# Recurrent attention and a channel-mixing layer in one kernel: decay scans in four parts, early bf16 fillers, late guards and a rewritten order

## The chip, the cores and the metric

One core of one Trainium2 chip. The metric is device microseconds (us) of one execution of the whole program. TensorE (PE) multiplies matrices into PSUM; VectorE (DVE), ScalarE (ACT) and GpSimd (POOL) do the elementwise work; the queue of SyncE (SP) issues all DMA transfers.

## The reference

Four batches, 8 heads, 768 time steps, head dimension 48. A linear recurrence with a decay gives `x`; a low-rank mix over time is added; two dense layers with a ReLU follow. All of it is float32.

```python
for t in range(S):                                   # S = 768
    cur = einsum('bhd,bhe->bhde', u[None] * kt, vt)
    y[:, :, t] = einsum('bhd,bhde->bhe', rt, state + cur)
    state = wt[..., None] * state + einsum('bhd,bhe->bhde', kt, vt)
x = y.transpose(0, 2, 1, 3).reshape(B, S, H * D)     # (4, 768, 384)
h = x.transpose(0, 2, 1) @ U @ V                     # U (768, 32), V (32, 768)
u = x + h.transpose(0, 2, 1)
out = u + maximum(u @ w_ch1, 0.0) @ w_ch2            # 384 -> 1536 -> 384
```

## The kernel before, in words

**Chunks.** Time is cut into 24 chunks of 128 steps (6 of each batch, `g` is 0 to 23). On the chip the recurrence of a chunk becomes matmuls. `chunk(g)` lays out the steps of one chunk. The decays `w` come as a 128 x 517 tile: four groups (head pairs) of 128 columns, each with a separator column in front. One scan over the whole tile (step `F`, `scan_f`, L380) multiplies the decays from the back; a second tile, `resets`, is 1 at the separators and 0 elsewhere and starts each group anew. Step `R` writes reciprocals of the four totals into the separator columns of `qd`, and a second scan over 516 columns (step `Q`, `scan_q`, L393) multiplies from the front. Step `T` keeps the totals, `RP` multiplies r by Q, `KS` multiplies k by F. `AM` (scores), `CP` (a predicated copy that merges the scores below a diagonal made by `SEL` and `SEL2`), `YA` and `YZ` (outputs from the chunk and from the state) follow. The state: `KT` and `KN` turn k, `DS` multiplies it with v into the PSUM tile `dS`, `ZA` adds the old state, `ZM` decays it. `XE` and `XN` take PSUM results to SBUF around the transposes `XT`. In batch 0 `PR`, `MD`, `DV` make the diagonal, in the others `RK`, `RU`, `RED`. `GUARD` (`check_w`, L409) reads the decays once more and counts those out of range; a branch at the end of the program reads the counts.

**Weights.** float64 weights come as raw tiles (`LRAW`) and are rebuilt as two tiles that the fast matmul format holds, a high and a low part: `AB`, `E`, `SG` (ACT, some on DVE), `C1`, `C2`, `ADD` (DVE, some on POOL), `HI` (ACT), `SUB` (POOL or DVE). There are 12 pieces of `w1`, 12 of `w2`, and one each of U and V.

**Dense layers.** Per batch and half of the time steps: 12 up projections (`UP`, 9 matmuls of 128x384 each, L782) and 12 parts of the down projection (`DN`, 9 matmuls each, L817); 96 of each in all, so 192 steps that are called dense steps below. `HH` and `HL` take the high and low part of the ReLU out of PSUM. The first of them needs all of batch 0's recurrence and its time mix: `GW` (6 parts) into `gb`, then `GS`, `GSL`, `IX`, `HP`, `UHP`, `ULP`, `XU`.

**Order.** Nothing is left to a scheduler. `ORDER` is a string with three characters for each step: two digits of base 64 are the step's number, the third says which of two engines takes it (odd: the step's `alt`) and, halved, how many units of filler matmuls go ahead of it (`warm`, L176: two units are one 128x512 matmul on a tile `busy`, an odd one is a 128x256 matmul; results are thrown away). `plan` (L122) reads it. Each engine runs its steps in that order, and a step waits until its inputs are there and its buffer is free.

Read out, the string has the first `UP` at place 373 of 1433. Ahead of it stand, by engine:

| engine | steps ahead of the first UP, before |
|---|---|
| DVE | F 9, Q 8, R 8, CP 8, PR 6, KS 5, RP 8, C1 16, C2 16, HI 1, ADD 10, SUB 6, SUBV 2, ZM 5, ZA 4, RK 2, RU 1, RED 2, GSL 1, ULP 3, UADD 1, DV 1 |
| ACT | GUARD 8, AB 16, E 16, SG 14, HI 11, SEL 5, SEL2 5, KN 7, XE 7, XN 6, T 8, DV 5, ZM 1, HIV 2, GS 1, UHP 3, XU 3 |
| POOL | KS 3, SEL 3, SEL2 3, ADD 4, SUB 6, RK 1, RU 1 |
| PE | MD 6, KT 7, AM 8, DS 7, YA 7, YZ 5, XT 6, GW 6, VM 2, IX 3, HP 4, and 95 filler units |

`busy` is the last part of the tile for the low half of `w2`, filled from `resets` by a conversion (L172); fillers can be placed until the step `GW 0.5`.

Of the kernel before, what the change touches and what calls it, by code (L numbers as in the profile page):

```python
# [39 lines left out]
def channel_order():  # L40
# [18 lines left out]
    "5y05405+06945s05E05A01D00Q05B14w01E05x10R00S05-04s02R01S08O05u05114t05F01F11k05v00m00o06A04-01G15C05D06015d6"
    "5e05J65w00p08R01z06115Z01H01I10q15G20r11+08T01-08Y05a18o05H02A06228X05b15c02006305K08y05Q05L04x04y02C05t18U0"  # L60
    "8Z00s00t02S05fC2B01U05h05I06B02D05M22T05g05N02E15i01T08P08z15r08a15j08p08b05k05l09h05m01V08W18V08Q06C02I09O0"
    "8r02a08c11W02U08t05n05o06408d16506602F02V08g08u01X18q06701Y06802W16D08v06E06F06G08+02K06H09g00I08e08f08x06I0"
    "6M01Z08S16J08-06N00J02X16R06S08w09208h09309008i02Y19409j08s18j06O06P06K06L06V02Z06T06U08k06Q09609P11a09F07M0"
# [979 lines left out]
```

## Time and profile before

| what | us |
|---|---|
| three runs: median (lowest, highest) | 459.84 (459.72, 462.23) |
| the profiled execution: span from the first to the last instruction | 458.4 |
| its own time beside the runs | the span is 1.4 below the median of the runs |
| busy: PE, DVE, ACT, POOL | 442.2, 296.7, 175.1, 104.5 |

Busy time is the time in which an engine had at least one instruction under way. Matmuls overlap, so a row's duration is longer than its share of the stream: 9 matmuls of 128x384 last 0.34 us each and follow each other in 1.59 us. On the other engines too the next instruction starts a little before the one in front has ended; the time from one start to the next is what an instruction takes of its engine.

### The profile page before, as it was taken

Reading aid. Unit: us, or ns where it says so; the run is one execution under the profiler, and the core shown is the slowest. Engines: PE = TensorE matmul, PEld = TensorE weight load, DVE = VectorE, ACT = ScalarE, POOL = GpSimd, SP = SyncE. Lnnn points to the kernel's source line nnn. Section 1 sums busy time; section 2 is a strip of 40 time slices with the busy share of each in tenths; the row PEclk is TensorE's granted clock in tenths of the full one; section 3 lists DMA queues with packets and bytes.
Section 4 is the critical chain, followed back from the end, with each engine's and each line's share of the span. In section 5 each row is a group of like instructions: output and inputs, shape, how many; then the busy total and the mean of one; then the engine's idle time right before and its main releaser. Section 6 shows DMA issues by size and latency. Waiting matters only on the chain.

```text
span 458.4 us, 9721 instructions
## 1 busy us (share of the span) xinstructions
PE 442.2 (96%) x4066; PEld 409.9 (89%) x4066; DVE 296.7 (65%) x529; ACT 175.1 (38%) x434; POOL 104.5 (23%) x99
## 2 busy tenths in 40 slices
PE   4998899999999999999999999999999999999996
PEld 3675668999999899899999799999998899999995
DVE  7998998999989584865865675672445235402511
ACT  5998997888545221333017100141122100101100
POOL 0222645343461160113522303222000010000000
PEclk9999999999999999999999999999999999999999
DMA  8946771584424524232414212041000000010001
GB/s 271 378 133 216 281 238 61 177 288 160 147 76 127 180 62 115 67 90 82 147 42 167 59 61 64 20 123 54 23 18 1 1 17 19 2 39 31 0 3 54
DMA packets 20497, 46.95 MB, mean 102 GB/s; under 512 B 2400, under 2 KB 8928, under 8 KB 20448
## 3 DMA queue, kind: packets, MB, share of 16 engines
q1 hardware_dynamic: 20448, 46.28, 30.4%
q8 instruction: 33, 0.54, 0.5%
q14 instruction: 16, 0.13, 0.1%
HBM read 41.55 MB, written 4.72 MB: 101 GB/s over the span
## 4 chain that ended last, share of the span: by engine, by line
PE 85%; DVE 7%; ACT 3%; DMA 2%; issue 1%; SPq 1%; DVEq 0%; ACTq 0%
PE f L782 33%; PE f L817 33%; PE aps L507 4%; PE y L566 2%; PE trk L495 2%; PE y L576 2%; PE trx L626 2%; PE y L589 1%; PE dS L517 1%; DMA rk<-in_rkT 1%; DVE A L510 1%; PE hp L723 1%; PE ga L649 1%; DVE Q L395 1%; PE idle L178 1%
## 5 line engine op out<-in xcount | busy, mean ns | idle before, releaser
L782 PE MATMUL f<-u,w1h 128*128 128x384 f32 x576 | 150.1, 341 | 0.7 <-ACT xT L745 0.7
L782 PEld LDWEIGHTS f<-u,w1h 128*128 128x128 f32 x576 | 103.7, 188 | 1.3 <-ACT xT L745 1.0
L817 PE MATMUL f<-hh,w2h 128*128 128x384 f32 x288 | 99.1, 344 | 0.0
L782 PE MATMUL f<-u,w1l 128*128 128x384 f32 x288 | 97.5, 339 | 0.0
L817 PE MATMUL f<-hh,w2l 128*128 128x384 f32 x288 | 97.4, 338 | 0.0
L817 PE MATMUL f<-hl,w2h 128*128 128x384 f32 x288 | 97.0, 337 | 0.0
L795 DVE SCALAR_TENSOR_TENSOR hl<-f,hh 128x384 fp32r<-128x384 f32 x96 | 52.4, 553 | 41.0 <-ACT hh L789 39.8
L789 ACT ACTIVATE hh<-f 128x384 fp32r<-128x384 f32 x47 | 23.1, 494 | 142.7 <-PE f L782 142.6
L817 PEld LDWEIGHTS f<-hh,w2h 128*128 128x128 f32 x288 | 54.1, 188 | 1.2 <-DVE hl L795 0.6
L817 PEld LDWEIGHTS f<-hl,w2h 128*128 128x128 f32 x288 | 54.5, 189 | 0.4
L782 PEld LDWEIGHTS f<-u,w1l 128*128 128x128 f32 x288 | 54.0, 188 | 0.0
L817 PEld LDWEIGHTS f<-hh,w2l 128*128 128x128 f32 x288 | 54.0, 187 | 0.0
L791 DVE TENSOR_SCALAR hh<-f 128x384 fp32r<-128x384 f32 x49 | 27.1, 554 | 33.4 <-PE f L782 33.4
L832 DVE TENSOR_TENSOR xT<-f,xT 128x384 f32<-128x384 f32 x24 | 13.0, 550 | 36.9 <-PE f L817 36.9
L510 DVE COPY_PREDICATED A<-maskf,aps 128x1024 f32<-128x1024 uint32 x24 | 32.7, 1361 | 2.8 <-PE aps L507 2.4
L445 ACT ACTIVATE A<-ident,dv 128x128 f32<-128x128 f32 x108 | 34.0, 394 | 1.2 <-DVE dv L435 1.2
L382 DVE TENSOR_TENSOR_SCAN F<-w,resets 128x517 f32<-128x517 f32 x24 | 30.7, 1281 | 4.4 <-DMA w<-in_wT 4.4
L395 DVE TENSOR_TENSOR_SCAN Q<-w,qd 128x516 f32<-128x516 f32 x24 | 31.1, 1295 | 0.2
L741 POOL TENSOR_TENSOR u<-xT,u 128x384 fp32r<-128x384 f32 x9 | 10.3, 1153 | 82.9 <-DVE u L737 63.8
L507 PEld LDWEIGHTS aps<-rk 48*128 48x128 f32 x384 | 23.3, 187 | 5.6 <-issue 3.9
L507 PE MATMUL aps<-rk 48*128 48x128 f32 x384 | 27.9, 285 | 0.5 <-DMA raw_w<-in_w 0.4
L407 POOL TENSOR_TENSOR rk<-rk,F 128x512 f32<-128x512 f32 x13 | 17.1, 1317 | 47.4 <-DVE F L382 27.5
(118 smaller groups left out, 586.7 us busy)
## 6 DMA issues: line engine op xcount, KB each, us to landing
rk<-in_rkT SPq DMA_DIRECT2D x24, 512.0 KB, 5.5
raw_w<-in_w SPq DMA_DIRECT2D x24, 384.0 KB, 5.5
kr<-in_rkN SPq DMA_DIRECT2D x18, 384.0 KB, 3.9
w<-in_wT SPq DMA_DIRECT2D x24, 258.5 KB, 3.4
v<-in_vN SPq DMA_DIRECT2D x24, 224.0 KB, 3.8
out_dram<-xT SPq DMA_DIRECT2D x24, 192.0 KB, 1.9
raw_U<-in_U SPq DMA_DIRECT2D x1, 192.0 KB, 2.8
raw_V<-in_V SPq DMA_DIRECT2D x1, 192.0 KB, 5.5
```

Source lines behind the costliest of these rows:

```text
L382: nc.vector.tensor_tensor_scan(out=F[:, ::-1], data0=st["w"][:, ::-1], data1=resets[:, ::-1], initial=1.0, op0=ALU.mult, op1=ALU.add)
L395: nc.vector.tensor_tensor_scan(out=st["Q"], data0=st["w"][:, 0:n], data1=qd, initial=0.0, op0=ALU.mult, op1=ALU.add)
L407: ENG[eng].tensor_tensor(out=rk[:, 1], in0=rk[:, 1], in1=F5, op=ALU.mult)
L445: nc.scalar.activation(A[:, i, j], ident, AF.Copy, scale=dv[:, NP * i + j : NP * i + j + 1])
L507: nc.tensor.matmul(aps[:, i, j, :], rk[r, 1, j, :], rk[r, 0, j, :], start=True, stop=True)
L510: nc.vector.copy_predicated(flat(st["A"]), mask8, flat(st["aps"]))
L782: nc.tensor.matmul(ps, wt[:, f, ct, :], u[ct][:, z], start=(n == 0), stop=(n == 8))
L789: nc.scalar.activation(hh, d["ps", f], AF.Relu)
L791: nc.vector.tensor_scalar(out=hh, in0=d["ps", f], scalar1=0.0, scalar2=None, op0=ALU.max)
L795: nc.vector.scalar_tensor_tensor(out=hl, in0=d["ps", f], scalar=0.0, in1=hh.bitcast(F32), op0=ALU.max, op1=ALU.subtract)
L817: nc.tensor.matmul(d["o", ct], wt[:, 4 * ct + part, f - 3 * part, :], hid[f][z], start=(part == 0 and n == 0), stop=(part == 3 and n == 8),)
L832: nc.vector.tensor_tensor(out=o, in0=d["o", ct], in1=o, op=ALU.add)
```

## The change

- **Scans.** `w` loses its separators (128 x 512). `F` and `Q` are four scans each, over 128 and 127 columns; the addend is a column of zeros, repeated, that lies in PSUM, in the same bank as `dS`. `R` writes its reciprocals into the first columns of the Q tile; these are the initial values of the four Q scans. `resets` and `qd` go; Q has two buffers.
- **Fillers.** `busy` is a bf16 tile of its own, set to zero by the first DVE instruction. Fillers can be placed until `HP 0.0.0`.
- **Guards of batch 0.** The six `GUARD` steps of batch 0 read `w` from a second load (`LG`) and stand late in the order (the last at place 1409 of 1439).
- **State of batch 0.** For chunks 1 to 4 the old state goes into PSUM by a matmul with the identity (`ZP`), `DS` adds to it there, and `ZM` reads PSUM; `ZA` goes.
- **Either engine.** `KN`, `XE`, `XN` may go to DVE.
- **Order.** A new string of 1439 steps. The first `UP` is at place 329. Ahead of it stand:

| engine | steps ahead of the first UP, after |
|---|---|
| DVE | F 9, Q 8, R 9, CP 7, PR 3, KS 2, RP 3, C1 12, C2 11, ADD 2, SUB 2, SG 1, SUBV 2, ZM 1, ZA 1, RK 2, RU 1, RED 2, GSL 1, ULP 3, XU 1, DV 1 |
| ACT | GUARD 2, AB 12, E 12, SG 10, HI 7, SEL 3, SEL2 3, KN 7, XE 6, XN 6, T 8, DV 5, ZM 5, HIV 2, GS 1, UHP 3, XU 1 |
| POOL | PR 3, RP 5, KS 7, SEL 5, SEL2 5, ADD 8, SUB 5, RU 1 |
| PE | MD 6, KT 7, AM 8, DS 7, ZP 4, YA 7, YZ 5, XT 6, GW 6, VM 2, IX 3, HP 3, and 49 filler units (31 of them ahead of MD 0) |

The diff, without the two strings and the lines that only rename:

```diff
-    resets = const.tile([P, NP * SEG + 1], F32, name="resets")
-    nc.vector.memset(resets, 0.0)
-    nc.vector.memset(resets[:, 0 : NP * SEG + 1 : SEG], 1.0)
+    busy = const.tile([P, 512], BF16, name="busy")
+    nc.vector.memset(busy, 0.0)
     ones = const.tile([P, 1], F32, name="ones")
-    nc.scalar.activation(ones, resets[:, 0:1], AF.Copy)
+    nc.vector.memset(ones, 1.0)
+    warmed = const.tile([P, 1], F32, name="warmed")
+    nc.scalar.activation(warmed, ones, AF.Copy)
...
-    busy = w2l.rearrange("p a b n -> p (a b n)")[:, -512:]
-    nc.vector.tensor_copy(busy, resets[:, 2:514])
-    dS = psS.tile([P, NP, ZW], F32, name="dS")
+    bank = psS.tile([P, 512], F32, name="bank")
+    dS = bank[:, 0 : NP * ZW].rearrange("p (j n) -> p j n", n=ZW)
+    zero = bank[:, NP * ZW : NP * ZW + 1]
+    nc.vector.memset(zero, 0.0)
+    zeros = zero.broadcast_to([P, P])
...
-    qd = const.tile([P, NP * SEG], F32, name="qd")
-    nc.vector.memset(qd, 0.0)
...
+        def load_w2():
+            st["w2"] = sb2.tile([P, NP, P], F32, tag="w", name=f"w2_{g}", bufs=W_BUFS)
+            nc.sync.dma_start(st["w2"].rearrange("p j t -> p (j t)"), wT[b, c])
...
         def scan_f():
-            F = st["F"] = sb2.tile([P, NP * SEG + 1], F32, tag="F", name=f"F_{g}")
-            nc.vector.tensor_tensor_scan(
-                out=F[:, ::-1], data0=st["w"][:, ::-1], data1=resets[:, ::-1], initial=1.0, op0=ALU.mult, op1=ALU.add
-            )
+            F = st["F"] = sb2.tile([P, NP, P], F32, tag="F", name=f"F_{g}")
+            for j in range(NP):
+                nc.vector.tensor_tensor_scan(
+                    out=F[:, j, ::-1], data0=st["w"][:, j, ::-1], data1=zeros, initial=1.0, op0=ALU.mult, op1=ALU.add
+                )
...
+        def first_q():
+            st["Q"] = sb2.tile([P, NP, P], F32, tag="Q", name=f"Q_{g}")
+            nc.vector.reciprocal(st["Q"][:, :, 0], st["F"][:, :, 0])
 
         def scan_q():
-            st["Q"] = sb2.tile([P, n], F32, tag="Q", name=f"Q_{g}", bufs=1)
-            nc.vector.tensor_tensor_scan(
-                out=st["Q"], data0=st["w"][:, 0:n], data1=qd, initial=0.0, op0=ALU.mult, op1=ALU.add
-            )
+            Q = st["Q"]
+            for j in range(NP):
+                nc.vector.tensor_tensor_scan(
+                    out=Q[:, j, 1:P], data0=st["w"][:, j, 0 : P - 1], data1=zeros[:, 1:P], initial=Q[:, j, 0:1],
+                    op0=ALU.mult, op1=ALU.add,
+                )
...
-        step("GUARD " + nm, "ACT", check_w, [lw], use=[buf["w"]])
+        if b == 0:
+            buf["w2"] = Buf("w")
+            lw2 = step("LG " + nm, "SP", load_w2, take=[buf["w2"]])
+            step("GUARD " + nm, "ACT", lambda: check_w("w2"), [lw2], use=[buf["w2"]])
+        else:
+            step("GUARD " + nm, "ACT", lambda: check_w("w"), [lw], use=[buf["w"]])
...
                     nc.tensor.matmul(
-                        dS[r, j, i * D : i * D + D], kn[:, j, r], v[:, j, r], start=True, stop=True
+                        dS[r, j, i * D : i * D + D], kn[:, j, r], v[:, j, r], start=not carry,
+                        stop=not carry or j == NP - 1,
                     )
+
+        carry = b == 0 and c > 0
+
+        def state_old():
+            flat_z = lambda t: t.rearrange("p j n -> p (j n)")
+            nc.tensor.matmul(flat_z(dS), ident, flat_z(old["Z"]), start=True, stop=False)
...
-            kn = step("KN " + nm, "ACT", copy_k, [kt], use=[buf["kn"], btr])
+            kn = step("KN " + nm, "ACT", copy_k, [kt], use=[buf["kn"], btr], alt="DVE")
...
+            if carry:
+                zp = step("ZP " + nm, "PE", state_old, [old["z"]], take=[buf["dS"]], use=[old["buf"]["Z"]])
+                ds = step("DS " + nm, "PE", state_add, [kn, lv, zp], use=[buf["dS"], buf["kn"], buf["v"]])
+            else:
+                ds = step("DS " + nm, "PE", state_add, [kn, lv], take=[buf["dS"]], use=[buf["kn"], buf["v"]])
+            from_ps = c == 0 or carry
+            zuse = [buf["dS"]] if from_ps else [buf["Z"]]
...
-    first, last = steps[0], next(s for s in steps if s.name == f"GW 0.{NCH - 1}")
+    first, last = steps[0], next(s for s in steps if s.name == "HP 0.0.0")
```

## Rows read from the trace of the kernel before

**Rows 1.** The page: busy time of each engine, its share, its instructions.
```profile
PE 442.2 (96%) x4066; PEld 409.9 (89%) x4066; DVE 296.7 (65%) x529; ACT 175.1 (38%) x434; POOL 104.5 (23%) x99
```

**Rows 2.** Stretches: length; busy PE, PEld, DVE, ACT, POOL; granted clock; DMA share; GB/s.
```profile
0.00:8.56 8.56, 2.07 (x4) 1.16 (x4) 6.04 (x17) 4.15 (x11) 1.00 (x7) 1.00 0.72 227
8.56:74.02 65.46, 60.07 (x797) 43.78 (x797) 62.47 (x110) 58.71 (x147) 25.52 (x20) 1.00 0.69 244
74.02:100.55 26.53, 26.53 (x277) 25.33 (x278) 25.57 (x51) 22.90 (x53) 9.49 (x9) 1.00 0.57 189
155.00:434.80 279.80, 279.78 (x2326) 269.59 (x2319) 149.59 (x254) 57.88 (x147) 48.53 (x45) 1.00 0.18 55
434.80:458.40 23.60, 19.26 (x110) 18.65 (x109) 3.88 (x12) 0.00 (x0) 0.00 (x0) 1.00 0.08 28
```

**Rows 3.** The chain of waits: start, us, what; ahead of the first UP.
```profile
66.38 0.57 DVE gs L668
67.43 0.65 PE hp L715 x2
74.02 14.58 PE f L782 x81
```

**Rows 4.** Timeline of DVE: start, duration, line, operation; from 3.69 to 42.
```profile
3.69 1.24 DVE L382 TENSOR_TENSOR_SCAN F<-w,resets 128x517 f32<-128x517 f32 x1
...
33.09 1.25 DVE L382 TENSOR_TENSOR_SCAN F<-w,resets 128x517 f32<-128x517 f32 x1
34.23 0.36 DVE L264 TENSOR_SCALAR cva_w<-cva_w 128x384 f32<-128x384 f32 x1
34.48 0.58 DVE L538 TENSOR_TENSOR Z<-dS,Z 128x384 f32<-128x384 f32 x1
34.95 0.20 DVE L418 RECIPROCAL qd<-F 128x4 f32<-128x4 f32 x1
35.03 1.34 DVE L510 COPY_PREDICATED A<-maskf,aps 128x1024 f32<-128x1024 uint32 x1
36.25 1.24 DVE L395 TENSOR_TENSOR_SCAN Q<-w,qd 128x516 f32<-128x516 f32 x1
...
40.24 0.68 DVE L407 TENSOR_TENSOR rk<-rk,F 128x512 f32<-128x512 f32 x1
40.84 0.69 DVE L402 TENSOR_TENSOR rk<-rk,Q 128x512 f32<-128x512 f32 x1
```

**Rows 5.** Timeline of ACT, same columns, from 38 to 42.
```profile
38.18 0.57 ACT L247 ACTIVATE cva_w<-raw_w 128x384 f32<-128x384 f32 x1
38.64 0.50 ACT L630 ACTIVATE xn<-trx 128x384 f32<-128x384 f32 x1
39.01 1.10 ACT L279 ACTIVATE raw_w<-raw_w 128x384 f16<-128x384 f32 x1
39.81 0.72 ACT L411 ACTIVATE junk<-w,b_max 128x512 uint8<-128x512 uint32 x1
40.49 1.28 ACT L445 ACTIVATE A<-ident,dv 128x128 f32<-128x128 f32 x4
41.66 0.49 ACT L609 ACTIVATE xT<-y 128x384 f32<-128x384 f32 x1
```

**Rows 6.** Timeline of POOL: one diagonal select each, beside a scan and without.
```profile
52.92 1.90 POOL L447 TENSOR_SCALAR_AFFINE_SELECT A<-dv 128x512 f32<-128x512 f32 x1
...
68.33 0.64 POOL L447 TENSOR_SCALAR_AFFINE_SELECT A<-dv 128x512 f32<-128x512 f32 x1
```

**Rows 7.** Timeline of DVE beside the first of these selects.
```profile
53.13 1.25 DVE L395 TENSOR_TENSOR_SCAN Q<-w,qd 128x516 f32<-128x516 f32 x1
...
55.15 1.17 DVE L271 TENSOR_SCALAR cva_w<-cva_w 128x384 uint32<-128x384 uint32 x1
```

**Rows 8.** Timeline of PE: the same eight matmuls of MD, early and later.
```profile
8.56 1.86 PE L468 MATMUL trd<-u_diag,kr 128*128 128x2 f32 x8 [2.67 <-DVE kr L463]
...
19.83 0.95 PE L468 MATMUL trd<-u_diag,kr 128*128 128x2 f32 x8
```

More of the change, by code (lines that the diff above doesn't have):

```diff
@@ L31 @@
 RANK = 32
-SEG = P + 1
 VW = 112
@@ L59 @@
[L59 to L63, printed above, removed]
@@ L156, in rwkv_moe_kernel, with copy @@
     dram = pool("dram", 1, space=DRAM)
+    def copy(eng, out, src):
+        if eng == "ACT":
+            nc.scalar.activation(out, src, AF.Copy)
+        else:
+            nc.vector.tensor_copy(out, src)
     hidp = pool("hidp", 24)
@@ L345, in chunk @@
         b, c = divmod(g, NCH)
[L346 removed]
+        st = sts[g] = dict(buf={p: Buf(p) for p in ("w", "rk", "kr", "v", "F", "Q", "A", "dv", "kn", "Z", "aps", "y", "dS", "xn")})
         buf = st["buf"]
@@ L409, in check_w @@
-        def check_w():
-            wv = st["w"][:, 0:n].rearrange("p (j s) -> p j s", s=SEG)[:, :, 1:SEG]
+            k = st["rk"][:, 1, :, 0 : P - 1]
+            ENG[eng].tensor_tensor(out=k, in0=k, in1=st["F"][:, :, 1:P], op=ALU.mult)
+        def check_w(which):
             nc.scalar.activation(
-                junk, wv.bitcast(U32), AF.Relu, bias=b_max, scale=2.0**-23, accum_out=guard[:, g : g + 1]
+                junk, st[which].bitcast(U32), AF.Relu, bias=b_max, scale=2.0**-23, accum_out=guard[:, g : g + 1]
@@ L551, in decay @@
                     )
-            if c > 0:
+            if not from_ps:
                 za = step("ZA " + nm, "DVE", add_z, [ds, old["z"]], take=[buf["Z"]], use=[buf["dS"], old["buf"]["Z"]])
             st["z"] = step(
-                "ZM " + nm, "DVE", decay, [ds] if c == 0 else [za],
-                take=[buf["Z"]] if c == 0 else [], use=zuse, alt="ACT",
+                "ZM " + nm, "DVE", decay, [ds] if from_ps else [za],
+                take=[buf["Z"]] if from_ps else [], use=zuse, alt="ACT",
             )
@@ L604, in chunk, with out_x @@
             xbuf[b, blk] = Buf("xT")
-        def out_x():
+        def out_x(eng):
             if cc == 0:
                 blocks[b, blk] = xtp.tile([P, NCT, TB], F32, tag="xT", name=f"xT_{b}_{blk}")
-            nc.scalar.activation(blocks[b, blk][:, :, cc * P : (cc + 1) * P], st["y"], AF.Copy)
+            copy(eng, blocks[b, blk][:, :, cc * P : (cc + 1) * P], st["y"])
         bx = xbuf[b, blk]
-        x = step("XE " + nm, "ACT", out_x, [y] + (xs_done[b, c - 1] if cc else []), take=[bx] if cc == 0 else [], use=[buf["y"], bx])
+        x = step("XE " + nm, "ACT", out_x, [y] + (xs_done[b, c - 1] if cc else []), take=[bx] if cc == 0 else [], use=[buf["y"], bx], alt="DVE")
         xs_done[b, c] = [x]
@@ L626, in go, with back @@
                 nc.tensor.transpose(tr[:, ct, :], blocks[b, blk][:, ct, cc * P : (cc + 1) * P], ident)
-        def back():
+        def back(eng):
             xn = d["xn"] = sb2.tile([P, NCT, P], F32, tag="xn", name=f"xn_{b}_{c}", bufs=NCH)
-            nc.scalar.activation(xn, d["tr"][:, 0:NCT, :], AF.Copy)
+            copy(eng, xn, d["tr"][:, 0:NCT, :])
         xt = step(f"XT {b}.{c}", "PE", go, after, take=[btr, bxn], use=[bx])
-        d["steps"] = [step(f"XN {b}.{c}", "ACT", back, [xt], use=[bxn, btr])]
+        d["steps"] = [step(f"XN {b}.{c}", "ACT", back, [xt], use=[bxn, btr], alt="DVE")]
         d["buf"] = bxn
@@ L997, in chunked @@
         return t
-    wT = np.zeros((B, NCH, P, NP * SEG + 1), f32)
-    wT[..., : NP * SEG].reshape(B, NCH, P, NP, SEG)[..., 1:] = chunked(w, 1.0)
+    wT = chunked(w, 1.0).reshape(B, NCH, P, NP * P)
     rkT = np.stack([chunked(r, 0.0), chunked(k, 0.0)], axis=3)
```

118 lines of the change are left out of this document (54 added, 64 removed).

## The prediction

> **What bounds the kernel now.** I read the shares first [rows 1]: PE is busy 96% of the span, DVE 65%, ACT 38%, POOL 23%. A share is an average, so next the stretches [rows 2]. From 74.02 on PE is full (26.53 of 26.53, then 279.78 of 279.80): whatever is removed from another engine there buys nothing. Ahead of that PE has only feeding work and fillers, and DVE is the full engine: 62.47 of 65.46, with ACT at 58.71 and POOL at 25.52. The chain of waits [rows 3] agrees: a mixed chain up to GSL (66.38) and IX, then one unbroken PE chain from 74.02. So there are two stages. In the first, 74 us, the end is set by DVE; in the second by the sum of PE's work. The change is worth what it takes off the first stage, unless it opens gaps in the second.
>
> **Unit prices, from one start to the next.** DVE [rows 4]: scan 1.14 (33.09 to 34.23), C1 0.25, a 384-column tensor operation 0.47, R 0.08, CP 1.22, a 512-column one 0.60. ACT [rows 5]: 384 columns 0.37 to 0.46, SG 0.80, GUARD 0.68, a select of four activations 1.17. POOL: 25.52 us for 20 instructions [rows 2], 1.28 each.
>
> These prices must first give the kernel before. DVE's list ahead of the first UP is 17 scans (19.4), 8 CP (9.8), 19 operations of 512 columns (11.4), 37 of 384 or like it (17.4), 33 C1, C2, HI (8.3), 9 small (0.7): 67.0. It had 74.02 - 3.69 = 70.3 [rows 3, 4], so it ran at 95% of its list. Counted to the thirteenth dense step (place of the first DN, 100.55), the same prices give 88.7 in 96.9, 92%.
>
> **The change, part by part.**
>
> *Scans in four parts.* From 384 to 512 columns a two-input operation grows by 0.13, so 0.08 of each is fixed, and a scan column costs (1.14 - 0.08) / 517 = 2.05 ns [rows 4]. A group of four is 4 x (0.262 + 0.08) = 1.37 for 1.14: +0.23 for each of the 17 groups of the first stage, +3.9 us on DVE. No row shows a scan with a PSUM addend. Below, 1.14, as if the parts had no fixed cost; less is excluded, since the columns stay and each hangs on the one in front. Above, each part may pay what R lasts, 0.20, as its fixed cost: 4 x 0.46 = 1.84, +12 us over 17 groups. PSUM as an input added nothing elsewhere: ZA, from PSUM, steps at 0.47 [rows 4]; so I take 1.37.
>
> *What the scans free.* A select on POOL beside a Q scan took 1.90 and one without a scan 0.64 [rows 6, 7], and right behind it a C2 took 1.17 where C1 lasts 0.36 [rows 4, 7]. POOL and DVE hold each other up when both read SBUF twice. Reading zeros from PSUM takes the scans out of that. But POOL goes from 20 to 39 steps, beside some 39 DVE operations that still read SBUF twice or in the fast mode. I take nothing off POOL's 1.28 and add 2 us to DVE (bounds: 0, and 39 x 0.2 = 8 if a quarter of that 0.8 us delay met each).
>
> *Work moved off DVE ahead of the first UP.* The new list: 17 scan groups (23.3), 7 CP (8.5), 8 of 512 (4.8), 19 of 384 (8.9), 23 C1 and C2 (5.8), 10 small (0.8): 52.1, 54.1 with the 2 us. Of the 13 us saved PR, RP and KS went to POOL (19 to 8), ADD and SUB to POOL or behind the first UP (16 to 4), five C1 and C2 each behind it, ZA to PE and ZM to ACT.
>
> *Guards late.* Six of 0.68 leave ACT's first stage, 4.1 us. They come back after 155, where ACT is busy 57.88 of 279.80, with 1.5 MB more of DMA where its share is 0.18 [rows 2]: nothing. Without that cover it would be the same 4 us. On SP's queue the six LG stand late; behind them wait only other late loads and the OUT transfers. Ahead of the first UP SP issues 49 transfers for 50, four raw tiles fewer and more of `rk`, `v` and `kr`; in 64 us for 74 the DMA share goes from 0.69 to about 0.80, still with room. The first ACT instruction no longer waits for `w`, but ACT's real work starts behind MD 0 and DV 0.
>
> *State by TensorE.* Four ZP; an IX, the same shape, is 0.65 in the chain [rows 3]: +2.6 us on PE in the first stage, where 65.46 - 60.07 is idle and more is filler [rows 2]. On ACT a ZM is four activations, as a select is [rows 5]: 1.17 each, five of them instead of one.
>
> *Fillers.* 95 units become 49, 31 of them before MD 0. A matmul of 384 columns is 0.18 (14.58 / 81) [rows 3], a unit of 256 columns 0.12. MD 1 took 1.86 at 8.56 and MD 0 0.95 at 19.83 [rows 8], with the granted clock shown as 1.00 in both, so PE was slow at first. With PE at work from about 1.5 us MD 0 may start fast: at most 0.9 us, on a stage that DVE and ACT set. Nothing.
>
> **The sum.** When can the first UP start? DVE: 3.7 + 54.1 / 0.95 = 60.6. POOL, from the landing of the first rk tile at about 5.5 (an estimate: one transfer earlier than in the trace, where MD 1 follows at 8.56): 5.5 + 39 x 1.28 / 0.95 = 58.0. ACT: 24 AB and E 11.0, SG 8.0, selects 7.0, ZM 5.9, KN and HI 6.4, XE and XN 4.4, guards 1.4, the rest 4.1, in all 48.2; its start behind MD 0 lies between 7.0 and 10.4 (end of MD 1 in rows 8), I take 8.2: 8.2 + 48.2 / 0.95 = 58.9. PE: 60.07 less 87 units (10.4), plus ZP 2.6 and 18 units (2.2), is 54.5 from about 7: 61.5. All four come out at 58 to 61.5, where before DVE stood alone.
>
> With less done ahead, the debt is paid behind it. To the thirteenth dense step DVE has 20 scan groups (27.4), 9 CP (11.0), 8 of 512 (4.8), 55 of 384 (25.9), 47 C (11.8), 11 small (0.9), with 2 for POOL: 83.8. At 95% that ends at 91.9, at 92% at 94.8. PE needs 28 us from the first UP to there (twelve UP 19.1, and 9 of scores, outputs and turns). So PE, full from the first UP on, may not start before 63.9 or 66.8, or has that much in gaps: 64.0 is the start that counts, for 74.02. The rest of PE's list is the same within 0.3. Gain 10.0 - 0.3, less 0.7 for new gaps later (an estimate: half a scan group, once) = 9.0. Span 458.4 - 9.0 = 449.4; the median of the runs lies 1.4 above the span: **450.8**.
>
> **Rivals.**
>
> *The four engines hold each other up* (0.17). Where one engine was full, a wait of another cost nothing; now each wait counts. With parts at 1.84 and the list at 92%: (83.8 + 20 x 0.47) / 0.92 + 3.7 - 28 = 77 as the worst; half way, 70.5: gain 2.5, 457. For it: the 92% above. Against: POOL and PE have no such sums behind the first UP.
>
> *Scans and state matmuls take turns* (0.07, the slower side). The zeros lie in the bank that DS and ZP write. If each must wait until the other is done with the bank, PE, which is full, stops for a scan group in front of DS. Place: 13 DS behind the first UP. Price: 13 x 1.37 = 17.8, against a gain of 9: 469. It decides from 0.7 us a DS. Against: only DS 12 has under 1.4 us of PE work between it and the last scan ahead of it in the string. The Trainium skill's page "PSUM — Partial Sum Buffer", section "PSUM bank collisions raise a hardware error", says that two engines may not touch one bank and quadrant in the same cycle, whatever the columns, and that software has to guard by bank. By that rule the turns exist; no row of before has a reader of `dS` beside a writer.
>
> *The scans still hold POOL up* (0.06). Then a scan group blocks it as in rows 6, 1.26 us for some 8 of 17 groups: 10 us on POOL, 58.0 to 68.5: gain 5, 455.
>
> *PE slows down for want of fillers* (0.03). At the price of rows 8 (1.86 for 0.95) the 54 us of PE would double; the gain is gone from 10 us of it at the lower clock. Against: PE's list fills the stage to 85% without them.
>
> *All at the low ends* (0.07): scans 1.14, no POOL delay: 83.8 - 4.6 - 2 = 77.2 / 0.95 + 3.7 - 28 = 57: bounded by PE's 61.5, 446.
>
> **How the numbers follow.** The forecast has 0.60: 447 to 454. The range 445.5 to 458 takes in the low ends, the POOL case and half of the first rival. A measurement of this kernel tells about 1% from no change (455.2 to 464.4). Faster: 0.60 + 0.07 + 0.05 of POOL + 0.06 = 0.78; same 0.13; slower 0.09.
>
> **What would show it.** First UP at 60 to 66; DVE, ACT, POOL and PE all over 85% busy ahead of it; a scan part stepping at 0.34; selects on POOL at 0.64 beside scans; no PE gap in front of DS; PE full from the first UP, save a few us before the first DN. The prediction is wrong if PE has gaps of more than 5 us in its first 30 us of UP, or if a scan part steps over 0.45.

## The result and the profile after

| | median of the runs (lowest, highest), us | span profiled | first UP | first DN | end of PE |
|---|---|---|---|---|---|
| before | 460.26 (459.32, 462.23), 10 runs | 458.4 | 74.02 | 100.30 | 454.06 |
| after | 463.91 (461.79, 467.19), 10 runs | 463.1 | 68.02 | 99.80 | 458.55 |
| forecast | 450.8 | 449.4 | 64.0 | 92.0 | 445.1 |

The ratio is 1.0076 with the 95% interval [1.005, 1.0101]. Under 2% a difference counts as no change here, but the interval leaves out 1: the kernel is 3.7 us slower as measured, 13.1 us above the forecast and outside its range. The first UP came 6.0 us earlier. By the first DN all but half a microsecond of that was gone (the first DN of before starts at 100.30, not at the 100.55 that the prediction read), and behind it PE took 5.0 us more than before to its end (358.7 for 353.8). An execution over 1.5% above the fastest of its kernel counts as slow: none of before and after, but three of six of e10 and one of six of e11 below, whose medians take them in.

The page's first part, and the stretches (length; busy PE, PEld, DVE, ACT, POOL; granted clock; DMA share; GB/s), cut where [rows 2] is cut by role, at the first UP and the first DN:

```profile
PE 442.9 (96%) x4046; PEld 406.6 (88%) x4049; DVE 308.4 (67%) x653; ACT 165.2 (36%) x406; POOL 122.7 (27%) x127
```

```profile
8.50:68.02 59.52, 51.41 (x753) 37.31 (x754) 54.63 (x122) 47.08 (x124) 39.57 (x39) 0.94 0.73 245
68.02:99.80 31.78, 28.64 (x302) 26.18 (x299) 31.17 (x61) 26.57 (x56) 17.70 (x17) 1.00 0.45 144
99.80:155.00 55.20, 52.38 (x415) 49.96 (x415) 42.96 (x90) 29.36 (x72) 15.87 (x16) 0.97 0.39 133
155.00:255.00 100.00, 99.79 (x962) 94.17 (x961) 72.93 (x159) 23.62 (x63) 32.43 (x33) 1.00 0.28 91
```

In [rows 2] PE is full from the first UP on (26.53 of 26.53). Here it is busy 28.64 of 31.78 us up to the first DN while DVE has 31.17 of 31.78, and PE is full only behind 155. DVE still sets the pace after PE's dense work has begun. What PE waits for, 68 to 160 us (total, times, longest):

```profile
PE f L805 <- DVE hl L818: 5.6, 5, 1.9
PE f L840 <- DVE w2l L343: 0.4, 1, 0.4
```

HL reads the PSUM tile of an UP last, so a late HL on DVE keeps the next UP out of PSUM. Five such gaps are 5.6 us. Why HL is late is seen on DVE, 72 to 82 us, and on POOL beside it (start, duration, line, operation):

```profile
72.69 1.03 DVE L443 TENSOR_TENSOR kr<-kr,u_rep 128x384 f32<-128x384 f32 x1
73.65 1.65 DVE L343 TENSOR_TENSOR w1l<-cva_w,w1h 128x384 fp32r<-128x384 f32 x1
75.22 0.35 DVE L271 TENSOR_SCALAR cva_w<-cva_w 128x384 f32<-128x384 f32 x1
75.49 0.55 DVE L818 SCALAR_TENSOR_TENSOR hl<-f,hh 128x384 fp32r<-128x384 f32 x1
...
77.15 1.34 DVE L393 TENSOR_TENSOR_SCAN F<-w,bank 128x128 f32<-128x128 f32 x4
78.41 2.13 DVE L271 TENSOR_SCALAR cva_w<-cva_w 128x384 f32<-128x384 f32 x2
80.46 1.49 DVE L278 TENSOR_SCALAR cva_w<-cva_w 128x384 uint32<-128x384 uint32 x2
```

```profile
72.29 1.03 POOL L343 TENSOR_TENSOR w1l<-cva_w,w1h 128x384 fp32r<-128x384 f32 x1
73.27 1.61 POOL L414 TENSOR_TENSOR rk<-rk,Q 128x512 f32<-128x512 f32 x1
...
78.14 1.01 POOL L343 TENSOR_TENSOR w1l<-cva_w,w1h 128x384 fp32r<-128x384 f32 x1 [0.63 <-ACT w1h L336]
79.11 1.21 POOL L418 TENSOR_TENSOR rk<-rk,F 128x508 f32<-128x508 f32 x1
80.28 1.46 POOL L459 TENSOR_SCALAR_AFFINE_SELECT A<-dv 128x512 f32<-128x512 f32 x2
```

A subtraction on DVE that lasts 0.55 alone takes 1.65: it starts at 73.65, POOL's product ends at 74.88, DVE's operation at 75.30. Two C1 take 2.13 and two C2 1.49, where one alone lasts 0.35 and the next may start after 0.25. HL of 75.49 stands behind all of the first group, and PE waits from 75.00 to 76.09. The scan group in between steps as ever: 1.26 us for four.

How much this is up to the first DN, by operation (count, busy us and mean ns, idle time before and what ended it), 4 to 100 us:

```profile
L407 DVE TENSOR_TENSOR_SCAN Q<-w,Q,bank 128x127 f32<-128x127 f32 x40 | 15.8, 457 | 2.3 <-ACT Z L570 1.2 <-PE bank L529 0.8
L393 DVE TENSOR_TENSOR_SCAN F<-w,bank 128x128 f32<-128x128 f32 x40 | 13.4, 397 | 2.5 <-DMA w<-in_wT 0.9 <-PE bank L529 0.7 <-PE bank L538 0.6
L271 DVE TENSOR_SCALAR cva_w<-cva_w 128x384 f32<-128x384 f32 x18 | 10.7, 610 | 0.3 <-ACT cva_w L254 0.2
L278 DVE TENSOR_SCALAR cva_w<-cva_w 128x384 uint32<-128x384 uint32 x17 | 7.3, 440 | 0.1
L295 DVE CUSTOM_DVE_ANT_0 cva_w<-raw_w,cva_w 128x768 uint16<-128x768 uint16 x7 | 4.6, 661 | 0.0
L343 DVE TENSOR_TENSOR w1l<-cva_w,w1h 128x384 fp32r<-128x384 f32 x4 | 4.5, 1118 | 0.0
```

Against 0.35 (C1, C2) and 0.55 (the other two) this is 18 x 0.26 + 17 x 0.09 + 7 x 0.11 + 4 x 0.57 = 9.3 us in four rows. Below, the *excess* is this sum over all operations: what each DVE instruction lasted beyond the tenth percentile of its line, tile and shape in the same trace, where that is over 0.05 us. Up to the first DN it is 10.7 us (before: 2.3), 5.1 of it ahead of the first UP (before: 2.0); from there to 160 us it is 6.5 more (before: 1.4). All 10.7 us lie on instructions that overlap a POOL instruction, and of the 85 scan parts and other operations with a PSUM input that overlap one none has an excess. A late POOL alone does not explain it: up to the first DN no DVE instruction waits for a result of POOL, and PE and ACT wait 0.6 and 0.8 us for one.

PE itself was slow twice: its granted clock is 1.00 from 6.10 us, 0.50 (1.2 GHz, the lower level) from 12.93 to 19.76 and again from 142.64 to 146.05, right behind the gap of 1.92 us at 140.41. The runs bear it out: the after run at a mean clock of 1.000 took 461.79, the one at 0.979 467.19.

### The profile page after: what moved, and what is told of

The parts are those of the page before. It is cut to its first block, busy times and chain, and to the rows that moved or that the text cites. A ratio compares the mean times of both kernels' runs of the same rounds, so it can differ in the third digit from the quotient of the medians.

```text
span 463.1 us, 9864 instructions
## 1 busy us (share of the span) xinstructions
PE 442.9 (96%) x4046; PEld 406.6 (88%) x4049; DVE 308.4 (67%) x653; ACT 165.2 (36%) x406; POOL 122.7 (27%) x127
## 4 chain that ended last, share of the span: by engine, by line
PE 75%; DVE 18%; ACT 3%; issue 2%; DMA 1%; DVEq 0%; ACTq 0%; SPq 0%
PE f L840 29%; PE f L805 28%; PE aps L519 4%; DVE Q L407 3%; PE y L589 2%; DVE F L393 2%; PE bank L529 2%; PE y L599 2%; DVE A L522 1%; DVE hl L818 1%; PE y L612 1%; DVE cva_w L271 1%; DVE cva_w L278 1%; PE trx L649 1%; PE trk L507 1%
## 5 line engine op out<-in xcount | busy, mean ns | idle before, releaser
L812 ACT ACTIVATE hh<-f 128x384 fp32r<-128x384 f32 x55 | 27.0, 496 | 118.1 <-PE f L805 118.1
L459 POOL TENSOR_SCALAR_AFFINE_SELECT A<-dv 128x512 f32<-128x512 f32 x32 | 21.5, 679 | 85.0 <-PE y L599 45.9
L393 DVE TENSOR_TENSOR_SCAN F<-w,bank 128x128 f32<-128x128 f32 x96 | 32.3, 398 | 11.2 <-DMA w<-in_wT 6.5
L407 DVE TENSOR_TENSOR_SCAN Q<-w,Q,bank 128x127 f32<-128x127 f32 x96 | 38.0, 458 | 2.6 <-ACT Z L570 1.2
L814 DVE TENSOR_SCALAR hh<-f 128x384 fp32r<-128x384 f32 x41 | 22.4, 550 | 24.6 <-PE f L805 24.6
L522 DVE COPY_PREDICATED A<-maskf,aps 128x1024 f32<-128x1024 uint32 x24 | 31.3, 1304 | 5.7 <-PE aps L519 5.7
L519 PEld LDWEIGHTS aps<-rk 48*128 48x128 f32 x384 | 24.5, 195 | 6.1 <-issue 3.0
L519 PE MATMUL aps<-rk 48*128 48x128 f32 x384 | 29.1, 293 | 0.6 <-POOL rk L414 0.6
L414 POOL TENSOR_TENSOR rk<-rk,Q 128x512 f32<-128x512 f32 x14 | 21.8, 1558 | 27.1 <-DVE Q L407 21.5
```

The source lines that it names most:

```text
L393: nc.vector.tensor_tensor_scan(out=F[:, j, ::-1], data0=st["w"][:, j, ::-1], data1=zeros, initial=1.0, op0=ALU.mult, op1=ALU.add)
L407: nc.vector.tensor_tensor_scan(out=Q[:, j, 1:P], data0=st["w"][:, j, 0 : P - 1], data1=zeros[:, 1:P], initial=Q[:, j, 0:1], op0=ALU.mult, ...
L414: ENG[eng].tensor_tensor(out=rk[:, 0], in0=rk[:, 0], in1=st["Q"], op=ALU.mult)
L459: nc.gpsimd.affine_select(out=A[:, i], in_=dv[:, NP * i : NP * i + NP].unsqueeze(2).broadcast_to([P, NP, P]), pattern=[[0, NP], [1, P]], c ...
L519: nc.tensor.matmul(aps[:, i, j, :], rk[r, 1, j, :], rk[r, 0, j, :], start=True, stop=True)
L522: nc.vector.copy_predicated(flat(st["A"]), mask8, flat(st["aps"]))
```

## The experiments

| run | median us | ratio to before, 95% | first UP |
|---|---|---|---|
| e1 short POOL steps | 454.74 | 0.9871 [0.9844, 0.9897] | 62.66 |
| e9 e1 and e8 together | 452.25 | 0.9829 [0.9812, 0.9847] | 64.43 |
| e5 before, 19 POOL products more | 473.74 | 1.0279 [1.0252, 1.0306] | 84.67 |
| e6 before, POOL fills instead | 468.73 | 1.0185 [1.0161, 1.021] | 79.90 |
| e13 zeros in SBUF | 475.97 | 1.0327 [1.0305, 1.0349] | 79.58 |
| e2 whole scans | 483.04 | 1.0475 [1.0442, 1.0508] | 74.18 |
| e3 before, scans in parts | 474.26 | 1.028 [1.0251, 1.031] | 86.82 |
| e10 e3 and 44 fillers | 476.43 | 1.035 [1.032, 1.0381] | 80.83 |
| e7 22 POOL steps back on DVE | 471.73 | 1.0252 [1.0219, 1.0285] | 74.31 |
| e15 state by DVE | 469.45 | 1.0198 [1.0175, 1.0221] | 75.60 |
| e4 24 fillers more | 462.99 | 1.0047 [1.0025, 1.0069] | 66.75 |
| e14 before, early fillers | 463.32 | 1.0068 [1.005, 1.0086] | 74.13 |
| e8 e4 and HL first | 459.04 | 0.9968 [0.9952, 0.9984] | 66.82 |
| e16 e8 and four moves more | 458.64 | 0.9956 [0.9937, 0.9976] | 66.87 |
| e11, e12 two new orders | 466.50, 472.50 | 1.0153 [1.0117, 1.0188], 1.0253 [1.0231, 1.0276] | 66.99, 78.94 |

By the bound of 2%, e2, e3, e5, e7, e10, e12 and e13 are slower than before, e6 and e15 unclear, and the others no change, though every interval leaves out 1. The median of before beside these runs was 460.10 to 460.42 each time, so the changed kernels can be compared with each other. e1 and e9 leave work out and are no kernels to use.

In e2, e3, e7, e12, e13 and e15 the granted clock also stood at 0.50 for 14 to 24 us ahead of the first UP (after: 6.8), so their times hold the loss of the part together with that of the clock.

Theory 1: POOL's new load and DVE hold each other up, so HL is late. Rival 2: the parts of the scans are too dear. Rival 3: the clock, for want of fillers.

### POOL's two-input steps shortened (e1)

```diff
- k = st["rk"][:, 1, :, 0 : P - 1]
- ENG[eng].tensor_tensor(out=k, in0=k, in1=st["F"][:, :, 1:P], op=ALU.mult)
+ nj, n = (1, 1) if eng == "Pool" else (NP, P - 1)
+ k = st["rk"][:, 1, 0:nj, 0:n]
+ ENG[eng].tensor_tensor(out=k, in0=k, in1=st["F"][:, 0:nj, 1 : 1 + n], op=ALU.mult)
...                                                     # RP, RK, RU, ADD likewise; SUB: a memset
```

> The changed kernel, with POOL's two-input operations cut to one column (RP, KS, RK, RU and ADD of w1 and w2) or turned into a fill that reads nothing (SUB); PR and UL stay whole. It leaves these products, sums and differences out. Theory 1 (POOL's new load holds DVE up): DVE's excess over its undisturbed durations, 17 us up to 160 us, falls below 5; the first UP starts at 63 to 66 for 68.02; PE's gaps behind it fall from 6.2 to under 2 us; 452 to 456 us. Rival 2 (the four-part scans are too dear): the scan groups still step at 1.27 and 1.55, DVE is still the late one, gaps of 4 us and more stay; 460 to 463. Rival 3 (the granted clock): it still falls at about 13 us and near 143 us, and the time stays above 461.

454.74, 9.2 less than after; first UP 62.66, first DN 91.45. The excess up to 160 us is 4.2 for 17.3. PE's gaps behind the first UP are 2.8 us for 6.2, not under 2 as expected. The scan parts last as long as before (399 and 458 ns), C1 does not:

```profile
L411 DVE TENSOR_TENSOR_SCAN Q<-w,Q,bank 128x127 f32<-128x127 f32 x40 | 15.8, 458 | 4.2 <-PE bank L537 2.4 <-ACT Z L578 1.2 <-PE bank L546 0.5
L278 DVE TENSOR_SCALAR cva_w<-cva_w 128x384 uint32<-128x384 uint32 x22 | 8.3, 393 | 0.2
L271 DVE TENSOR_SCALAR cva_w<-cva_w 128x384 f32<-128x384 f32 x22 | 8.0, 375 | 0.7 <-ACT cva_w L254 0.6
```

Theory 1, and not rival 2. The clock stayed at 1.00 as well; e4 bounds its part. The run also makes POOL's own results early. But the first DN comes 8.4 us earlier and the excess up to it is 8.1 us smaller (2.6 for 10.7), while DVE waited for no result of POOL in either kernel: most of the gain is what DVE was held up. e5 and e6 part the two further.

### POOL's load put on the kernel before (e5, e6)

```diff
  s.run()
+ if s.eng == "Pool" and n_pool[0] < 19:
+     n_pool[0] += 1
+     nc.gpsimd.tensor_tensor(out=spill, in0=four, in1=four, op=ALU.mult)   # e6: three memsets of spill
```

> The kernel before, with one product of two SBUF tiles (512 columns, nobody reads its result) added on POOL behind each of its first 19 POOL steps, as much as the change adds to POOL. Theory 1 (POOL's load holds DVE up): C1, C2, HI and the two-input DVE operations beside POOL go from 0.35 and 0.55 to 0.7 and more, DVE's excess up to 74 us rises by 19 x 0.3 = 5 to 6 us, and since DVE sets the first stage of the kernel before, the first UP goes from 74.0 to 78 to 81: 464 to 467 us. If POOL's load costs DVE nothing (rivals 2 and 3): 460 to 461.5 us.

> As the run with 19 added POOL products in the kernel before, but each product is replaced by three fills of the same tile, which read nothing. If it is the reading of SBUF on two engines that holds DVE up: DVE's excess up to 68 us stays near 2 to 4 us (12.7 with the products), the first UP starts at 74 to 77, 460 to 463 us. If it is POOL's own queue that gets late: POOL is as busy as with the products, and the first UP starts above 80 again, 468 us and more.

Products: 473.74, first UP 10.7 us later, about twice what theory 1 forecast. Fills: 468.73, which lies in the range given for a late queue of POOL, with the first UP 5.9 later and just short of the 80 named there. Yet POOL is no less busy with the fills than with the products (47.4 and 44.7 us up to the first UP), and the delay is half as long. It goes with the excess up to the first UP: 14.3 and 7.4 us, 12.3 and 5.4 more than before's 2.0. What differs is which DVE operations are hit, e5 first, then e6, 4 to 100 us:

```profile
L395 DVE TENSOR_TENSOR_SCAN Q<-w,qd 128x516 f32<-128x516 f32 x10 | 13.9, 1391 | 0.0
L264 DVE TENSOR_SCALAR cva_w<-cva_w 128x384 f32<-128x384 f32 x16 | 8.6, 549 | 0.0
```

```profile
L395 DVE TENSOR_TENSOR_SCAN Q<-w,qd 128x516 f32<-128x516 f32 x10 | 12.2, 1218 | 0.0
L264 DVE TENSOR_SCALAR cva_w<-cva_w 128x384 f32<-128x384 f32 x16 | 10.2, 642 | 3.4 <-ACT cva_w L247 3.4
```

Q scans, which read SBUF twice, are at 1.22 on average with the fills and at 1.39 with the products (F scans: 1.23 and 1.27). C1, one input in the fast mode (384 columns step at 0.25 us, where two inputs take 0.47 [rows 4]), is held up by both. One and the same product RP on DVE, in e5 beside an added product, then in e6 beside fills (DVE, then POOL):

```profile
20.19 1.44 DVE L402 TENSOR_TENSOR rk<-rk,Q 128x512 f32<-128x512 f32 x1
20.03 1.05 POOL L979 TENSOR_TENSOR spill<-ident 128x512 bf16<-128x512 f32 x1
```

```profile
20.25 0.68 DVE L402 TENSOR_TENSOR rk<-rk,Q 128x512 f32<-128x512 f32 x1
20.08 1.68 POOL L979 MEMSET spill<- 128x512 bf16 x3
```

Up to the first UP, of the operations that overlap fills alone, 4 of 7 in the fast mode (C1, C2) are held up and none of 16 with two SBUF inputs, scans among them. Of those that overlap added products alone, both in the fast mode and all 4 with two SBUF inputs are held up, and none of 3 with a PSUM input. The Trainium skill's page "SBUF — State Buffer", section "SBUF: two separate sides", says just this: the two engines share one pair of ports as an exclusive lock for a whole instruction, taken by DVE's fast mode against any POOL operation, and by its operations with two SBUF inputs only against a POOL operation that reads SBUF. These counts agree with both halves. The prediction knew the contention and not that it can last to the end of the other's instruction.

### Zeros in SBUF; whole scans (e13, e2)

```diff
- zero = bank[:, NP * ZW : NP * ZW + 1]
+ zero = const.tile([P, 1], F32, name="zero")          # e13
```

> The changed kernel with one edit: the column of zeros that the scans add lies in SBUF and not in the bank of the state. If the zeros from PSUM are what keeps the scans clear of POOL (theory 1), scan parts beside a POOL step now last longer than 0.40 and 0.46, POOL's selects and products beside scans go from 0.64 and 1.28 to 1.5 and more, the first UP comes 3 to 7 us later, 466 to 472 us. If the turns in the bank cost more than that (the forecast's second rival), DVE no longer waits for PE's state matmuls nor PE for scans (2.1 and 1.2 us up to 100 us), and the time falls to 460 to 462.5.

> The changed kernel with each scan in one piece again (separators in the tile, resets and first values from SBUF, one Q tile and one tile of first values for two Q tiles; a few loads and scans of later batches moved back in the order for that); all the rest as changed. Rival 2 (the parts are too dear): DVE gets 20 x 0.29 = 5.8 us back up to the first DN, the first UP starts at 64 to 66, the gaps behind it fall below 2 us; 456 to 459 us. Theory 1 (POOL and DVE hold each other up): whole scans read SBUF twice again, so POOL steps beside them go to 1.9 us and scans to 1.4 to 1.9; what DVE saves in columns it loses again; first UP 67 to 71, 462 to 468 us.

e13: 475.97, 12 us over after, more than expected. A scan part goes from 397 to 684 ns on average; excess up to 68 us 17.9, all but 0.2 of it on scans. The rows of DVE, 4 to 100 us, and one F group of 3.69 us beside four POOL steps:

```profile
L407 DVE TENSOR_TENSOR_SCAN Q<-w,Q,zero 128x127 f32<-128x127 f32 x40 | 25.2, 688 | 0.1
L393 DVE TENSOR_TENSOR_SCAN F<-w,zero 128x128 f32<-128x128 f32 x40 | 25.0, 684 | 1.7 <-DMA w<-in_wT 1.1 <-issue 0.3 <-ACT tots L159 0.2
```

```profile
28.44 3.69 DVE L393 TENSOR_TENSOR_SCAN F<-w,zero 128x128 f32<-128x128 f32 x4 [0.33 <-issue]
```

POOL's selects beside scans are at 0.75, not at the 1.5 and more that were expected: here it is mostly DVE that waits. The waits of DVE on the bank are gone; what that saved is far less than the loss. e2, whole scans in the new order, 483.04: scans 1.69 and 1.59 on average (1.14 from start to start in [rows 4]), POOL's diagonal selects 0.90 for 0.73. PE's gaps of 9.5 us at 286 to 314 us lie in later batches, where the order had to be moved for the single Q tile; the first stage alone is 6.2 us longer than after.

### The parts alone in the old order (e3, e10)

```diff
- out=st["Q"], data0=st["w"][:, 0:n], data1=qd, initial=0.0, op0=ALU.mult, op1=ALU.add
+ out=Q[:, j, 1:P], data0=st["w"][:, j, 0 : P - 1], data1=zeros[:, 1:P], initial=Q[:, j, 0:1],
+ op0=ALU.mult, op1=ALU.add,                            # F likewise; e10: 44 more filler units
```

> The kernel before, in its own order and with its own fillers, with the four-part scans and the zeros from PSUM alone (tiles without separators, a second Q tile). Rival 2 (the parts cost what their columns and starts say): 17 scan groups at 1.43 for 1.14 put 4.9 us on DVE ahead of the first UP, some 2 us come back from selects and C2 that no longer run beside whole scans: first UP at 76 to 78, 462.5 to 464.5 us. Other outcome (what the scans free on POOL and behind it is worth more than the parts cost, as the whole scans in the new order were far dearer): first UP at 70 to 73, 456 to 459 us.

> The kernel before with the four-part scans alone, with 44 more filler units ahead of KT, AM, YA and DS between 12 and 70 us. Without them the granted clock fell to 0.5 for 24 us of that stretch and the time was 474.3. If the clock made most of that loss, it now stays at 1.0 up to the first UP, which starts at 78 to 81, 464 to 467 us: what is left is the price of the parts on DVE. If the parts themselves did it (DVE's list, or turns in the bank), the time stays above 471.

e3 fell outside both outcomes: 474.26. From 8.5 to 66 us DVE was busy only 47.24, and PE ran at a clock of 0.78 and 0.81:

```profile
8.50:40.00 31.50, 26.00 (x237) 19.91 (x237) 27.55 (x68) 23.98 (x60) 6.66 (x5) 0.78 0.67 243
40.00:66.00 26.00, 25.18 (x287) 18.57 (x283) 19.69 (x46) 18.96 (x50) 7.38 (x9) 0.81 0.50 173
```

PE is busy only 2.05 of 4.00 us from 18 to 22 (before: 3.56), its clock falls at 22.68, and then DVE waits for PE (4.9 us for the score matmuls). That the parts on DVE start this is argued; PE's waits there are 0.6 us for DVE and 1.3 that the trace puts down to a load. With more fillers the profiled execution kept a clock of 0.999 and took 468.75, first UP 80.83: 6.8 us later than before, 0.40 for each of 17 scan groups where 0.23 was forecast. That is no pure price of the parts: DVE still waits 3.6 us for score matmuls, and the fillers are work of PE too. Two more executions took 473.68 and 475.39, three fell to 0.977 and took 477.5 to 477.9. So the price of the parts in this order has only an upper bound, from the one execution at the full clock, and more fillers did not hold the clock.

### The moved steps (e7, e15)

```
e7:  in the first 512 places, 10 ADD and 12 SUB of the weights change their digit: POOL -> DVE
e15: carry = False                                      # ZA for ZP in batch 0
```

> The changed kernel with 22 of its POOL steps ahead of the first DN (10 ADD and 12 SUB of the weights) given back to DVE at the same places of the order. Theory 1 (a POOL step costs DVE 10.7 / 19 = 0.56 us by the run with added products, about what the same operation costs on DVE, 0.47): the first UP moves by under 2 us either way and the time is 461 to 466. By the forecast's price (2 us for 39 POOL steps, 0.05 each): 22 x 0.42 = 9 us later, 470 us and more.

> The changed kernel with batch 0's state added by DVE again (four ZA for four ZP). By the forecast's prices DVE gets 4 x 0.47 = 1.9 us more in the stage that it sets and PE 2.6 us less: first UP 1 to 2 us later, 464.5 to 466.5 us. If PE's chain (ZP, its turn in the bank, DS, ZM) is the late one, 461 to 463.

e7 refutes my own price: 471.73, first UP 6.3 us later. Excess up to 100 us falls only from 10.7 to 7.8, 0.13 for each POOL step; on DVE the same step is 0.47. In e5 DVE still holds the whole scans and the products that the change has moved away, so more of its list is exposed than here; that this makes the 0.56 of e5 is argued, not shown. The move to POOL is worth 8 us even with its contention, what the clock lost in e7 included (13.7 us at 0.50 for 6.8).

e15: 469.45, 5.5 us slower than after. DVE's four additions are 1.9 of it at most; more is their wait for PE, with all the rest of DVE queued behind them, and the clock (23.9 us at 0.50). Where the additions stand in the order was not searched again, so part of this can be their place:

```profile
DVE Z L561 <- PE bank L529: 8.7, 5, 3.9
```

### Fillers (e4, e14)

```
e4:  24 more units ahead of MD 1, DS 0, VM V1, MD 2, YA 0, AM 1
e14: before, with busy as a bf16 tile and 22 more units ahead of MD 1
```

> The changed kernel with 24 more filler units (0.12 us each) ahead of MD 1, DS 0, VM V1, MD 2, YA 0 and AM 1, between 9 and 18 us. Rival 3 (the clock that falls from 12.9 to 19.8 us costs the time): the granted clock stays at 1.0 there, the first UP comes 2 to 3.5 us earlier, 460 to 461.5 us. Theory 1: the clock may stay up, but DVE sets the first UP: it moves by under 1 us either way, and the time is 462.5 to 465.

> The kernel before with the early fillers alone: a bf16 tile of zeros filled first, and 22 more units ahead of MD 1, so that PE works from about 1.5 us. The forecast put this part at nothing: the clock is up when MD 1 starts, MD 1 takes 0.95 for 1.86, but DVE sets the stage: first UP within 0.7 us of 74.0, 459.5 to 461. If PE's first steps are on the path, 457.5 to 459.

e4: the clock stays at 1.00 up to the end of the dense steps, 462.99, 0.9 less; first UP 1.3 earlier. Rival 3 is worth one microsecond of the median, two at most (461.79 was the run of after at the full clock). e14: the profiled execution has its first UP at 74.13 and took 460.01, as forecast; six others at mean clocks of 0.978 to 0.985 took 463 to 465. In the profiled one the clock is up for MD 1 (1.06 for 1.86) but down again from 9.4 to 12.8 us (0.95 for 8.5 to 40; before, it is 1.00 from 15.3 us on and stays). An early start of the fillers does not pay by itself.

### What stands in front of HL (e8, e9, e16)

```
e8:  e4, and HH 7, HL 7 ahead of SUB w1.3; HH 0, HL 11, HL 0, HL 3 ahead of C2 w1.10;
     HL 3 of the second half ahead of RED 10
e16: e8, and HH 6, HL 6, HH 5 ahead of ADD w2.3; C1 w2.3 behind HL 3
```

> The changed kernel with the 24 added fillers and seven steps moved forward in the order: HH and HL of UP 7, HH 0 and HL 11, 0, 3 of the first block, HL 3 of the second, each ahead of the splits and scans that stood in front of it on DVE. If the gaps of PE are a matter of what stands in front of HL: the gaps at 73.7, 82.0 and 139.3 us (1.1, 1.4 and 1.9 us) go, 458.5 to 460.5 us. If DVE as a whole is late (theory 1): the first two come back elsewhere ahead of the first DN, only the last goes: 461 to 462.

> POOL's two-input steps shortened (as in the first run, with the same work left out), together with the 24 added fillers and the seven steps moved forward. If contention, the order in front of HL and the clock are separate terms that add up, their effects so far (9.2, 4.0 and 0.9 us off 463.9) leave 449 to 451.5, the time that was forecast; if they overlap (a DVE that is not held up needs no other order), 452.5 to 455.

> The changed kernel with the added fillers and the seven steps moved forward, and four more moves where its trace shows a loss: HH 6, HL 6 and HH 5 of the first block ahead of ADD w2.3 (1.32 us beside a POOL step, PE's gap of 1.04 us at 85.7 ends with that HL), and C1 w2.3 (1.17 us beside a POOL step) behind HL 3. If the order in front of HL is what is left, that gap goes and the time falls by 1 to 1.5 us, from 459.0 to 457.5 to 458; if DVE as a whole sets the pace up to the first DN, it stays at 459.

e8: 459.04, 4.0 under e4. PE's waits for HL fall from 5.6 to 2.4 us, and the first DN comes 1.6 us earlier than in e4:

```profile
PE f L805 <- DVE hl L818: 2.4, 3, 1.0
```

e16: 458.64; the gap at 85.7 is gone, one of 1.09 is back at 89.7, and one of 1.03 at 109.6 waits for a piece of w2. So both outcomes are half right: the order was worth 4 us, and the rest moves on, since DVE as a whole is late. Both kernels are faster than after, and by their intervals 0.3 and 0.4% faster than before, under the bound of 2%. e9 takes POOL's work away as well: 452.25, no gap above 0.2 us behind the first UP, PE full from there on:

```profile
64.43:92.12 27.69, 27.69 (x302) 26.37 (x300) 25.84 (x61) 26.19 (x56) 5.72 (x18) 1.00 0.52 167
```

The terms overlap by 2.4 us: 463.91 - 9.2 - 0.9 - 4.0 would be 449.8.

### Two orders made for less contention (e11, e12)

> The changed kernel with the 24 added fillers, the same steps and the same operations, but with the first 720 steps in a new order and about 80 of them on the other engine that may do them, so that DVE's operations on two SBUF tiles or in the fast mode stand less often beside a POOL step, and HL and HH stand first. If what DVE loses to POOL (16 us up to 160 us) and what stands in front of HL set the time, DVE's excess falls to 8 to 12 us, the first UP starts at 61 to 65, PE's gaps are under 4 us: 449 to 455 us. If something else does (the clock, the bank), 458 and more.

e12 is another order of the same aim, expected at 449 to 455 and within 3 us of e11. Both missed: e11 took 466.50 (461.31 at a clock of 0.994, the others 465 to 471 at lower clocks), e12 472.50. The excess up to 100 us fell to 7.8 and 7.9. But up to 160 us it is 11.2 in e11 and 17.4 in e12, for 17.3 in after: e12 only moved the contention and tests nothing. In e11, which met its aim, PE waits 4.1 us up to 70 us for scans in the bank (2.2 in one place, ahead of ZP) and 2.4 us for one up to 129, right ahead of a fall of the clock. In e12 the clock fell three times ahead of the first UP. Less contention alone is not enough where an order opens other waits.

## Why the prediction was wrong

**The step that failed** is the one sentence on POOL: "I take nothing off POOL's 1.28 and add 2 us to DVE (bounds: 0, and 39 x 0.2 = 8 ...)". The excess measures 10.7 us up to the first DN, 8.4 more than the 2.3 of before that the divisors 0.95 and 0.92 already hold: four times the 2 us, and just over the upper bound. Behind the first DN it is 6.5 us (before: 1.4), where nothing was reckoned. The mechanism named was right; its size was not. The bound was built on a quarter of one delay per POOL step. The rows show that one of the two engines waits for the end of the other's instruction: of the 40 fast-mode and two-input operations of DVE that meet a POOL instruction up to the first DN 20 are held up, by 0.5 us on average, and at others POOL is. With POOL's two-input work taken away and HL in front (e9), the excess up to the first DN is 2.1 us, as the forecast had it, and the forecast's own marks appear: first UP 64.43 for 64.0, first DN 92.12 for 92.0, end of PE 445.5 for 445.1. So DVE's list and the choice of DVE as the bound stand. POOL and ACT were priced too high: 39 steps of POOL take 39.57 us, 1.01 each for 1.28, and ACT is 79% busy ahead of the first UP where over 85% was forecast.

**"Less 0.7 for new gaps later"** was the second. PE's gaps behind the first UP are 6.2 us, 5.6 of them waits for HL. Moving HL in front of splits and scans (e8) took away 3.2 us of these and 4.0 us of the time. The prediction summed DVE's list up to the thirteenth dense step and never asked in what order HL comes in it.

**The balance.** The span is 13.7 us above the forecast's 449.4: the first UP is 4.0 later, the gaps are 5.5 more than the 0.7, and the lower clock near 143 us costs about 1.7 (half of 3.41, an estimate). The other 2.5 us are not assigned.

**Scans at 1.37.** F groups step at 1.26, Q groups at 1.50, 1.38 on average; the part steps at 0.31 and 0.37, near the 0.34 named. Right as a price. In the old order at the full clock (e10) the first UP came 6.8 us later for the 3.9 of 17 groups, with waits for PE in it.

**What the scans free** was right and undersold: selects beside scans last 0.64, and zeros in SBUF cost 12 us, the clock's loss included (e13). The case that scans still hold POOL up is refuted.

**Turns in the bank**, the slower rival: up to 100 us DVE waited 2.1 us on PE for the bank and 1.2 on ACT, not 13 scan groups. It was not the cause. The waits exist, and e11 shows them grow with another order.

**Fillers "Nothing".** MD 0 took 0.95 at 7.04, as said. But the clock fell at 12.93, and this costs some 1 to 2 us of the median (e4); the slowest of the ten executions is also the one at the lowest clock.

**State by TensorE** was costed at PE's 2.6 against DVE's four additions; in this order it is worth 5.5 us, since it takes a wait for PE out of DVE's list (e15). **Guards late** were not tried alone; ACT was never the bound (47.08 of 59.52).

**The rival "the four engines hold each other up"** (0.17) came nearer, with a first UP at 70.5 and 457 us, though it too was a gain; its price, dearer parts and a list at 92%, was not the one. **All at the low ends**: its 61.5 for the first UP gives about 447.6 by the forecast's own sum, not the 446 written.

**The signs of being wrong** did not show it: PE's gaps in its first 30 us of UP are 3.1 us, under the 5 named, and the parts step at 0.31 and 0.37, under 0.45. The first UP at 68.02, outside 60 to 66, did.

What stays open: the exact share of POOL's earlier results in the 9.2 us of e1 (waits for POOL are 1.4 us on PE and ACT together, up to the first DN), the 2.5 us of the balance, and what makes the clock of one and the same kernel fall in some executions only.

## What to carry to other kernels

Before moving work from DVE to POOL, list which DVE operations will stand beside it: in these runs fast-mode ones and those with two SBUF inputs were held up for as long as the POOL step lasted, or held it up themselves, and those with a PSUM operand were charged nothing. Where a chain of engines feeds PE, the step that frees PE's PSUM tiles (here HL) goes in front of whatever has time. A sum of busy times finds the bound of a stage, but not whether the one short step that PE waits for comes early in it.
